# A fused attention and MLP-mixer kernel: mixing products take PSUM banks of two pools by turns, and three transposes move ahead

## The chip, the cores and the metric

The kernel runs on one core of one Trainium2 chip. The metric is device time in microseconds (us) of one execution; the time of a version is the median of its runs.

## The reference

Inputs are q, k, v of shape (8, 12, 448, 64), two gains g_q, g_k of 64 values, and four weight matrices, all float32. Per batch element ("element" below, numbered 0 to 7):

```
q_n, k_n = rmsnorm(q) * g_q, rmsnorm(k) * g_k          # per row of 64
attn = softmax(q_n @ k_n.T / 8) @ v                    # 12 heads of 448 x 448
x = attn with heads side by side                       # 448 x 768
u = x + (relu(x.T @ w_tok1) @ w_tok2).T                # token mixing, 256 wide
out = u + relu(u @ w_ch1) @ w_ch2                      # channel mixing, 1536 wide
```

## The kernel before, in words

The whole program is one pipeline over the 8 elements. While the channel mixing of element b runs on TensorE (PE), the attention of element b+1 is laid between its products, so that PE has matmuls all the time and VectorE (DVE), ScalarE (ACT) and GpSimd (POOL) work beside it. The order on those four engines is the order in which the Python code emits the work; the order of the DMA issues on SyncE (SP) is made by a scheduler. In the trace each engine, and SP's queue, works through its list in that order, so whatever stands behind a waiting instruction waits too.

**Channel mixing.** Both channel products are done with fewer, fast-matrix products than the plain way. For elements 1 to 7 the first layer is 21 units `ch1` (L1131; three groups `mp` of seven products `i`, six matmuls each, 128x224). Element 1 has a plain second layer, `plain_2` (L1185: six products, each two units of six 448-wide matmuls). Elements 2 to 7 have 15 products `ch2` (L1199; two units `x` = 0, 1 of four matmuls each), called f = 0 to 14 below. A product's result stands in a PSUM tile `m_ps`; it is read ("evicted") by DVE at L1149, L1197 or L1224, or copied by ACT at L1153, L1165 or L1220. Some evicted values are combined on DVE or POOL (L1183, `x_form`) into the moving operands of later products: the tables `X_STEPS` and `X_SLOT` say which slot of `hb` is formed after which unit, and which slot a product reads. Slot 8 is formed anew on POOL after unit (7, 1) and read by product f = 11. Weights come as "units" by DMA (L1071) into eight buffers.

**PSUM pools.** The code divides PSUM into eight tiles of 128x512, called banks here: `ps_M` (L140) has 2, for the products (`m_tile`), and `ps_S` (L138) has 4, for the scores and small transposes (`s_tile`); the other 2 are for attention's outputs, `o_ps`. A tile can only be written when the last reader of the tile before it in its bank is done.

**Attention of the next element.** For two pairs of heads and one block of 64 keys, `score` (L453) takes two `s_tile`s, runs four 64x64-tiled matmuls (L459), and ACT takes the exponential out of each tile (L463). DVE sums these (`es`, L500). q and k of a pair are loaded by SP into `qk_t` (L1563, eight DMAs a pair), squared by ACT (L1585), reduced by DVE (L1598), put through three Newton steps for the inverse root (L1620 on DVE, then L1628 to L1631, on DVE or on POOL), scaled (L1649), and turned by DVE (`turn_qk`, L436) and ACT (L439). The buffers `qk_t` are two, for even and odd pairs.

For elements 2 on, the attention of the next element comes in six blocks (`big_step`, L625), set between units of the mixing by `place` (L675) at the units `BLOCKS = (0, 6, 11, 17, 23, 31)`. A block is a run of scores and values on PE; its third list, `beside`, follows it at once, and the fourth, `between`, is spread over the units up to the next block. For block 4 (a second_block, L646) `between` holds: the turns of one more pair, the loads of the pair after next (`loads(n + 2)`, first set below), four DVE steps, the loads of `n + 3` (second set below), and two more steps. Block 5 is a first_block; its two squares read the first and the second set.

**x for the next element.** Attention's output stands transposed. `x_items(b + 1, 0)` turns half of it (three DVE transposes, `trans_x`, L878), after which `send_x` stores it to DRAM (`xs`, four DMAs, L836) and `load_x` reads it back as `x` (five DMAs, L849 and L852), all on SP; `x_items(b + 1, 1)` does the other half later. The call that puts the first half into the list of block 4 is the line

```
blocks[4][3].extend(x_items(b + 1, 0))
```

Of the kernel before, what the change touches and what calls it, by code (L numbers as in the profile page):

```python
# [83 lines left out]
def whole(ctx, tc, shifted, pre, q, k, v, g_q, g_k, moe_w_tok1, moe_w_tok2, moe_w_ch1, moe_w_ch2, out):  # L84
# [67 lines left out]
    st = dict(pre.st)  # L152
    m_tile = lambda: ps_M.tile([P, 512], F32, name="m_ps", tag="M")
    s_tile = lambda name: ps_S.tile([P, 512], F32, name=name, tag="S")

    first_ps = s_tile("first_ps")
    for _ in range(7):
# [932 lines left out]
    def put_off_done():  # L1090
        while late_work:
            late_work.pop(0)()
# [38 lines left out]
    def ch1(b, mp, i):  # L1131

        put_off_done()
        u, tu = st["uT", b], st["tu"]
        ps = m_tile()
        w = next_unit()
        q, what = PRODUCTS[i]
        for j in range(2):
            for t in range(KC):
                m = {"B11": u[:, t, 0:HS], "B21": u[:, KC + t, 0:HS], "B22": u[:, KC + t, HS:S]}.get(what)  # L1140
                if m is None:
                    m = tu[:, int(what[1]) - 1, t, :]
                nc.tensor.matmul(  # L1143
                    out=ps[:, j * HS:(j + 1) * HS], lhsT=w[:, t, j, :], rhs=m,
                    start=(t == 0), stop=(t == KC - 1))
        got = ps[:, 0:2 * HS]
        h = {name: hb[:, 2 * mp + n, 2 * o:2 * o + 2, :].rearrange("p m n -> p (m n)")
             for name, o, n in (("B11", 0, 0), ("B12", 0, 1), ("B21", 1, 0), ("B22", 1, 1))}
        add = lambda e, o, x, y: e.tensor_tensor(out=o, in0=x, in1=y, op=ALU.add)  # L1149
        relu = lambda name: put_off(lambda: nc.scalar.activation(out=h[name], in_=h[name], func=AF.Relu))  # L1150
        if i == 0:
            r[1] = r_tile(1)[:]
            nc.scalar.copy(out=r[1], in_=got)  # L1153
        elif i == 1:
            add(nc.vector, h["B11"], got, r[1])
            relu("B11")
        elif i == 2:
            r[2] = r_tile(2)[:]
            add(nc.vector, r[2], got, r[1])
        elif i == 3:  # L1160
            r[3] = r_tile(3)[:]
            add(nc.vector, r[3], got, r[2])
        elif i == 4:
            r[5] = r_tile(5)[:]
            nc.scalar.copy(out=r[5], in_=got)  # L1165
            add(nc.gpsimd, h["B22"], r[5], r[3])
            add(nc.gpsimd, r[2], r[2], r[5])
            relu("B22")
        elif i == 5:
            add(nc.vector, h["B12"], got, r[2])  # L1170
            relu("B12")
        else:
            add(nc.vector, h["B21"], got, r[3])
            relu("B21")
        if b > 1 and mp == KF // 2 - 1:
            for form in X_STEPS.get(("ch1", i), ()):
                x_form(*form)
# [7 lines left out]
    def plain_2(b, mt, half):  # L1185

        put_off_done()
        if half == 0:
            st["m"] = m_tile()
        ps, w = st["m"][:, 0:S], next_unit()[:].rearrange("p a b n -> p (a b) n")  # L1190
        for t in range(KF):
            nc.tensor.matmul(  # L1192
                out=ps, lhsT=w[:, t, :], rhs=natural(half * KF + t),
                start=(half == 0 and t == 0), stop=(half == 1 and t == KF - 1))
        if half:
            to = st["uT", b][:, mt, :]
            nc.vector.tensor_tensor(out=to, in0=to, in1=ps, op=ALU.add)  # L1197

    def ch2(b, f, x):  # L1199

        put_off_done()
        if x == 0 or ending(b) and f == NF9 - 1:
            st["m"] = m_tile()
        ps = st["m"]
        for i in range(4):
            tile_at = f * 8 + x * 4 + i
            if tile_at % 6 == 0:
                st["w"] = next_unit()[:].rearrange("p a b n -> p (a b) n")
            nc.tensor.matmul(  # L1209
                out=ps[:, x * HS:(x + 1) * HS], lhsT=st["w"][:, tile_at % 6, :], rhs=hb[:, X_SLOT[f], i, :],  # L1210
                start=(i == 0), stop=(i == 3))
        if x:
            u = st["uT", b]
            at = {(m, n): u[:, m:m + KC + 1:KC, n * HS:(n + 1) * HS] for m in range(3) for n in range(2)}
            wide = lambda a: a[:, 0:2 * HS].rearrange("p (m n) -> p m n", m=2)
            at["P"] = wide(ps)
            for eng, out, x_, op, y in C_STEPS[f] if not (ending(b) and f == NF9 - 1) else ():
                if op is None:
                    r[out] = wide(r_tile(out))
                    nc.scalar.copy(out=r[out], in_=at["P"])  # L1220
                    continue
                e = nc.gpsimd if eng == "g" else nc.vector
                get = lambda k: at[k] if k in at else r[k]
                e.tensor_tensor(  # L1224
                    out=get(out), in0=get(x_), in1=get(y), op=ALU.add if op == "+" else ALU.subtract)
        if ending(b) and f == NF9 - 1:
            part = st["uT", b][:, 1 + x * KC, 0:HS]
            nc.vector.tensor_tensor(out=part, in0=part, in1=ps[:, x * HS:(x + 1) * HS], op=ALU.add)
        for form in X_STEPS.get((f, x), ()):
            put_off(lambda form=form: x_form(*form))  # L1230
# [43 lines left out]
    def x_items(b, h):  # L1274
        return [(0.1, lambda j=j: trans_x(b, j)) for j in range(h * NC // 2, (h + 1) * NC // 2)]
# [115 lines left out]
    for b in range(B):  # L1391
        early, double = middle_items(b)
        if b == 0:
            early, last = first_items(
                tok1_items(0, 0) + x_items(0, 1) + tok1_items(0, 1) + early, double, some)
        else:
            if b > 1 and in_next(b - 1):

                y, z = sends(b - 1, y_order(b - 1)[:4]), left
                left = [y[0], y[1], z[0], y[2], z[1], y[3]]  # L1400
            run(merge(tok1_items(b, 0), left[:2]))
            begin, early = merge(tok1_items(b, 1) + early[:3 * KC], left[2:]), early[3 * KC:]
            if b == 1 and not shifted:
                run(merge(begin, sums[5:9]))
                early, begin = merge(early[:8], sums[9:]) + early[8:], []
            elif b == 1:
                early, begin = merge(begin + early[:8], sums[5:]) + early[8:], []
            if b == 1:
                form_items()
            tail, keep = (4, 2) if b == 1 else (14, 3) if ending(b) else (11, 6)  # L1410
            last, ends = double[-tail - keep:-tail], double[-tail:]
            double = double[:-tail - keep]
            early = begin + early + double
        lo = (b + AHEAD) * per + 1
        att = []
        if b + AHEAD < B and (shifted or b < 2):
            att = att_items(lo, lo + 10) + x_items(b + AHEAD, 0)
            if shifted:
                att += att_items(lo + 10, lo + per)
            elif not b:  # L1420
                step = att_step(lo + per - 1)
                att += att_items(lo + 10, lo + per - 1) + step[:5] + x_items(1, 1) + step[5:]
            else:
                run(att[:6])
                ahead, block, beside, between = big_step(BIG, False)
                att = att[6:] + att_items(lo + 10, lo + per - 1) + ahead + [block] + beside
                att += between[:6] + x_items(2, 1) + between[6:-3]
                behind_x = between[-3:]
        elif b + AHEAD < B:
            t = (b + AHEAD) * NPAIR // 2  # L1430
            blocks = [big_step(t + i // 2, i % 2) for i in range(1, NPAIR + 1)]
            blocks[4][3].extend(x_items(b + 1, 0))
            early = place(early, blocks, [near(early, at) for at in BLOCKS], in_seven(b))
        if b == 0:
            last = x_items(1, 1) * shifted + merge(last, sums[:5], turns(b, y_order(b)[2:4]))
        else:
            if b + 1 < B:
                last = merge(last, behind_x if b == 1 and not shifted else x_items(b + 1, 1))
            if b == 2 and not shifted:
                last.append((0.4, right_sums))  # L1440
            last += last_items(b, ends)
        run(merge(att, early) + last)
        if b == 0:
            load_units(0)
        left = [] if b and ending(b) else turns(b, y_order(b)[4:])
# [275 lines left out]
```

## Time and profile before

| | |
|---|---|
| median of 3 runs | 1261.07 us (1258.13 to 1261.94) |
| the profiled execution's own time | 1262.04 us |
| its span, first to last instruction | 1260.2 us |
| busy: PE, DVE, POOL, ACT | 98%, 69%, 36%, 33% |
| element 1's mixing | about 275 to 417 us |
| elements 2, 3, 4, 5 | end at about 563, 709, 855, 1001 us |

An engine's busy share is a mean over the stages; the waits of PE by the engine that ended them say what delays it. A timeline row gives start, duration, engine, line, operation, tiles and how many instructions it merges; in square brackets stands the idle time of the engine just before, and what ended it.

### The profile page before, as it was taken

The page shows a single profiled execution, that of the slowest core. Times are in us where ns is not written, and L with a number is a line of the kernel's source. Part 1 is how long each engine was busy: PE and PEld are TensorE (multiplying, and loading weights), DVE is VectorE, ACT ScalarE, POOL GpSimd, SP SyncE. Part 2 cuts the span into 40 slices and gives each one's busy share as a digit, 9 for nine tenths or more (in the row PEclk, how much of TensorE's full clock was granted, in tenths as well). Part 3 has the DMA queues.
Part 4 walks back from the last instruction along what each step waited for, and adds up shares of the span by engine and source line. Part 5 has one row for each costly group of instructions (what it writes and reads, how often), then busy time and mean ns, then how long its engine had stood idle before and what let it go on. Part 6 is the DMA issues. An engine that isn't in the chain of part 4 may idle for free.

```text
span 1260.2 us, 20320 instructions
## 1 busy us (share of the span) xinstructions
PE 1234.3 (98%) x7196; PEld 900.9 (71%) x7196; DVE 867.8 (69%) x1379; ACT 412.2 (33%) x872; POOL 452.5 (36%) x681
## 2 busy tenths in 40 slices
PE   7999999999999999999999999999999999999998
PEld 4444444457744487797778877887787887798998
DVE  6989879757774466867688487866768486656243
ACT  5664443224332144402542044312444034301210
POOL 2311651033995922334224142344133242133222
PEclk9999999999999999999999999999999999999999
DMA  9666696899799887694767767685766956486564
GB/s 206 153 172 186 183 244 162 205 259 250 211 251 208 214 204 164 130 260 93 193 154 177 190 155 177 155 200 136 191 168 131 241 119 163 120 203 172 168 174 105
DMA packets 480275, 228.39 MB, mean 181 GB/s; under 512 B 362900, under 2 KB 440084, under 8 KB 480164
## 3 DMA queue, kind: packets, MB, share of 16 engines
q1 hardware_dynamic: 472626, 211.85, 68.5%
q0 software_dynamic: 4512, 14.46, 3.9%
q8 instruction: 59, 0.97, 0.3%
q10 hardware_dynamic: 3026, 0.69, 0.3%
q14 instruction: 52, 0.43, 0.1%
HBM read 184.26 MB, written 42.66 MB: 180 GB/s over the span
## 4 chain that ended last, share of the span: by engine, by line
PE 82%; DVE 7%; SPq 4%; DMA 3%; issue 2%; ACT 2%; DVEq 0%; ACTq 0%
PE m_ps L1143 26%; PE m_ps L1209 18%; PE s_ps L459 9%; PE o_ps L532 9%; PE m_ps L1113 5%; PE m_ps L891 3%; PE t_ps L891 2%; PE m_ps L1192 2%; PE m_ps L1023 2%; PE seven_ps L977 2%; DMA qk_t<-in_k_dram 2%; PE m_ps L977 1%; SPq L1563 1%; DVE es L500 1%; SPq L412 1%
## 5 line engine op out<-in xcount | busy, mean ns | idle before, releaser
L1209 PE MATMUL m_ps<-hb,unit 128*128 128x224 f32 x1440 | 277.0, 353 | 4.5 <-DVE uT L1224 4.5
L1209 PEld LDWEIGHTS m_ps<-hb,unit 128*128 128x128 f32 x1440 | 271.3, 190 | 12.8 <-issue 7.1
L1143 PE MATMUL m_ps<-tu,unit 128*128 128x224 f32 x1008 | 202.1, 355 | 2.4 <-DVE hb L1149 1.4
L1143 PEld LDWEIGHTS m_ps<-tu,unit 128*128 128x128 f32 x1008 | 188.9, 190 | 16.8 <-issue 7.8
L463 ACT ACTIVATE e<-s_ps 128x448 f32<-128x448 f32 x294 | 138.3, 553 | 130.4 <-PE s_ps L459 130.0
L1143 PE MATMUL m_ps<-uT,unit 128*128 128x224 f32 x756 | 151.5, 354 | 0.0
L1143 PEld LDWEIGHTS m_ps<-uT,unit 128*128 128x128 f32 x756 | 142.0, 190 | 7.2 <-POOL tu L1047 2.8
L459 PE MATMUL s_ps<-qkT 64*64 64x448 f32 x1260 | 144.3, 545 | 1.1 <-ACT x L873 1.1
L532 PE MATMUL o_ps<-e,v 64*64 64x448 f32 x1148 | 130.5, 538 | 0.1
L500 DVE TENSOR_TENSOR es<-es,e 128x896 f32<-128x896 f32 x90 | 106.1, 1179 | 13.8 <-ACT e L463 9.4
L1149 POOL TENSOR_TENSOR hb<-r,r 128x448 f32<-128x448 f32 x21 | 23.9, 1140 | 218.6 <-ACT r L1165 218.6
L459 PEld LDWEIGHTS s_ps<-qkT 64*64 64x64 f32 x1260 | 45.1, 132 | 69.4 <-issue 52.5
L532 PEld LDWEIGHTS o_ps<-e,v 64*64 64x64 f32 x1148 | 45.5, 133 | 63.9 <-issue 60.8
L1628 POOL TENSOR_TENSOR nt<-rs 128x56 f32<-128x56 f32 (+1 forms) x54 | 21.7, 402 | 181.8 <-DVE rs L1620 178.6
L1224 POOL TENSOR_TENSOR uT<-uT,r 128x448 f32<-128x448 f32 x42 | 54.6, 1315 | 86.6 <-DVE r L1224 49.6
L1149 DVE TENSOR_TENSOR hb<-m_ps,r 128x448 f32<-128x448 f32 x63 | 38.8, 618 | 64.9 <-POOL r L1149 45.0
L1598 DVE TENSOR_REDUCE ms<-sq 128x28 f32<-128x896 f32 (+2 forms) x44 | 47.0, 1069 | 48.4 <-ACT sq L1585 41.4
L1150 ACT ACTIVATE hb<-hb 128x448 f32<-128x448 f32 x84 | 48.4, 576 | 91.1 <-DVE hb L1149 76.9
L324 POOL TENSOR_TENSOR raw<-raw 128x128 f32<-128x128 f32 x128 | 67.3, 545 | 20.0 <-DMA raw<-wp 15.5
L1224 DVE TENSOR_TENSOR uT<-uT,m_ps 128x448 f32<-128x448 f32 x41 | 24.9, 618 | 53.8 <-PE m_ps L1209 53.8
L1220 ACT COPY r<-m_ps 128x448 f32<-128x448 f32 x24 | 12.7, 529 | 143.4 <-PE m_ps L1209 143.4
L1113 PE MATMUL m_ps<-hb,stage 128*128 128x448 f32 x144 | 57.1, 556 | 2.0 <-ACT r L1124 1.9
(183 smaller groups left out, 1797.1 us busy)
## 6 DMA issues: line engine op xcount, KB each, us to landing
unit<-ws SPq DMA_DIRECT2D x267, 384.0 KB, 4.3
raw<-in_moe_w_ch_dram SPq DMA_DIRECT2D x72, 256.0 KB, 3.5
v<-in_v_dram SPq DMA_DIRECT2D x96, 112.0 KB, 3.6
out_dram<-turned SPq DMA_DIRECT2D x182, 56.0 KB, 2.0
xs<-xt SPq DMA_DIRECT2D x52, 168.0 KB, 4.5
qk_t<-in_q_dram SPq DMA_DIRECT2D x144, 56.0 KB, 3.5
qk_t<-in_k_dram SPq DMA_DIRECT2D x144, 56.0 KB, 3.5
x<-xs SPq DMA_DIRECT2D x39, 192.0 KB, 3.9
```

The costliest lines, as they stand in the source:

```text
L324: nc.gpsimd.tensor_tensor(out=at[o], in0=at[x], in1=at[y], op=ALU.add if op == "+" else ALU.subtract)
L459: nc.tensor.matmul(out=pss[i][rows_of(i, a), 0:S], lhsT=qkT[h, 1, k * D:(k + 1) * D], rhs=qkT[h, 0, :], start=True, stop=True)
L463: nc.scalar.activation(out=e[:, i, :], in_=pss[i][:, 0:S], func=AF.Exp)
L500: nc.vector.tensor_tensor(out=es[:], in0=(es if k > 1 else st["e", t, 0])[:], in1=st["e", t, k][:], op=ALU.add)
L532: nc.tensor.matmul(out=st["o", p][a * D:(a + 1) * D, 0:S], lhsT=vt[rows, k * D:(k + 1) * D], rhs=e[rows, :], **kw)
L891: nc.tensor.matmul(out=st["t1", h][jc][:, 0:HC], lhsT=w1_sb[:, c, jc * P:(jc + 1) * P], rhs=st["x", b, h][:, :, c, :], start=start and c = ...
L1113: nc.tensor.matmul(out=ps, lhsT=a[:, o + 2 * half, :], rhs=natural(half * KF + t) if wide else u[:, half * KC + t, :], start=(t == 0 and h ...
L1143: nc.tensor.matmul(out=ps[:, j * HS:(j + 1) * HS], lhsT=w[:, t, j, :], rhs=m, start=(t == 0), stop=(t == KC - 1))
L1149: add = lambda e, o, x, y: e.tensor_tensor(out=o, in0=x, in1=y, op=ALU.add)
L1150: relu = lambda name: put_off(lambda: nc.scalar.activation(out=h[name], in_=h[name], func=AF.Relu))
L1209: nc.tensor.matmul(out=ps[:, x * HS:(x + 1) * HS], lhsT=st["w"][:, tile_at % 6, :], rhs=hb[:, X_SLOT[f], i, :], start=(i == 0), stop=(i == 3))
L1224: e.tensor_tensor(out=get(out), in0=get(x_), in1=get(y), op=ALU.add if op == "+" else ALU.subtract)
```

## The change

First, a new function `product_tile` counts the products and hands out a tile of `ps_M` for odd counts and one of `ps_S` for even ones. `ch1`, `plain_2` and `ch2` call it where they called `m_tile` (the branch `shifted` doesn't run here). Second, `x_items(b + 1, 0)` goes to the front of the `between` list of block 4 instead of its end. Five lines are added at the top, so every line below is numbered 5 higher in the changed kernel.

```
+    def product_tile():
+
+        st["bank"] = st.get("bank", 0) + 1
+        return m_tile() if shifted or st["bank"] % 2 else s_tile("m_ps")
...
-        ps = m_tile()
+        ps = product_tile()
...
-            st["m"] = m_tile()
+            st["m"] = product_tile()
...
-            blocks[4][3].extend(x_items(b + 1, 0))
+            blocks[4][3][:0] = x_items(b + 1, 0)
```

The order of PE's instructions is the same in both. DVE in element 3, behind block 4, before (`xt` is the transposed half of x, `ms` the reduced squares, `r_22476` a product's temporary):

```order
L1183 TENSOR_TENSOR hb<-hb 128x896
L436 STREAM_TRANSPOSE qkT<-qk_t 128x448 x2
L1224 TENSOR_TENSOR r_22476<-r_22476,m_ps 128x448
L1183 TENSOR_TENSOR hb<-hb 128x896
L500 TENSOR_TENSOR es<-es,e 128x896
L1224 TENSOR_TENSOR uT<-uT,m_ps 128x2x224
L500 TENSOR_TENSOR es<-es,e 128x896
L559 STREAM_TRANSPOSE dt<-es 128x448
L560 TENSOR_REDUCE v_first<-dt 128x14
```

DVE at the same place in the changed kernel:

```order
L1188 TENSOR_TENSOR hb<-hb 128x896
L883 STREAM_TRANSPOSE xt<-uT 128x448 x3
L441 STREAM_TRANSPOSE qkT<-qk_t 128x448
L1229 TENSOR_TENSOR r_22476<-r_22476,m_ps 128x448
L441 STREAM_TRANSPOSE qkT<-qk_t 128x448
L1188 TENSOR_TENSOR hb<-hb 128x896
L1229 TENSOR_TENSOR uT<-uT,m_ps 128x2x224
L505 TENSOR_TENSOR es<-es,e 128x896 x2
```

The three transposes of x now stand ahead of the turns of the pair (L441); before, they stood behind all the rows shown and eight more. SP's queue in element 3, before, from the first set's q on (`qk_t` are the loads of q and k, `unit` the weights, `xs` the stores of x; the other two stores and the loads of x come within six rows behind these):

```order
L1563 DMA qk_t<-in_q_dram 32x14x32 x4
L1563 DMA qk_t<-in_k_dram 32x14x32 x3
L1563 DMA qk_t<-in_q_dram 32x14x32
L1071 DMA unit<-ws_17248 128x768
L1563 DMA qk_t<-in_q_dram 32x14x32
L1071 DMA unit<-ws_17248 128x768
L1563 DMA qk_t<-in_q_dram 32x14x32
L1071 DMA unit<-ws_17248 128x768
L1563 DMA qk_t<-in_q_dram 32x14x32
L1563 DMA qk_t<-in_k_dram 32x14x32 x4
L1071 DMA unit<-ws_17248 128x768
L836 DMA xs<-xt 32x42x32 x2
```

SP's queue at the same place in the changed kernel, from the first stores of x on:

```order
L841 DMA xs<-xt 32x42x32 x2
L1076 DMA unit<-ws_17248 128x768
L1568 DMA qk_t<-in_q_dram 32x14x32
L1568 DMA qk_t<-in_k_dram 32x14x32
L841 DMA xs<-xt 32x42x32
L1568 DMA qk_t<-in_k_dram 32x14x32 x2
L841 DMA xs<-xt 32x42x32
L1076 DMA unit<-ws_17248 128x768 x2
L854 DMA x<-xs 128x3x128 x3
L857 DMA x<-xs 64x3x128 x2
L1568 DMA qk_t<-in_q_dram 32x14x32 x4
L1568 DMA qk_t<-in_k_dram 32x14x32 x3
```

The stores of x stand among the first set's loads, and the five loads of x stand ahead of the second set (the last two rows; its eighth load follows behind one unit). Before, the second set stood ahead of the stores and loads of x.

More of the change, by code (lines that the diff above doesn't have):

```diff
@@ L1202, in ch2 @@
         if x == 0 or ending(b) and f == NF9 - 1:
-            st["m"] = m_tile()
+            st["m"] = product_tile()
         ps = st["m"]
```

## The prediction

> **What bounds the kernel now.** The page comes first, then PE's own waits (who waited for whom: us in total, times, longest).
>
> ```profile
> span 1260.2 us, 20320 instructions
> PE 1234.3 (98%) x7196; PEld 900.9 (71%) x7196; DVE 867.8 (69%) x1379; ACT 412.2 (33%) x872; POOL 452.5 (36%) x681
> PE first_ps L158 <- DVE ms L1598: 9.4, 1, 9.4
> PE m_ps L1209 <- DVE uT L1224: 4.5, 4, 1.1
> PE m_ps L1143 <- DVE hb L1149: 1.4, 1, 1.4
> PE m_ps L1143 <- ACT r L1153: 0.7, 1, 0.7
> PE m_ps L1192 <- DVE uT L1197: 0.6, 1, 0.6
> ```
>
> PE sets the time: of 25.9 us without a matmul, 9.4 are the start. The last four rows are products that wait for a bank, 4.5 + 1.4 + 0.7 + 0.6 = 7.2 us: about all that the first edit can win. Any new wait of PE costs its whole length. The span and 1.8 us around it make the profiled 1262.04 us, 1.0 above the median, so terms worked out on this execution are added to the median.
>
> **The banks in element 1.** A product's bank used to come free with the eviction of the product two before. Every second product now takes a score bank, freed by ACT's exponential; in return a score may have to wait for a product's eviction. Which tile follows which is in the built program's addresses; when is in the timelines of ACT and PE:
>
> ```profile
> 290.24 0.67 ACT L439 ACTIVATE qkT<-qkT,g_t 128x448 f32<-128x448 f32 x1 [8.72 <-DVE qkT L436]
> 291.28 1.82 ACT L463 ACTIVATE e<-s_ps 128x448 f32<-128x448 f32 x4
> 285.63 1.73 PE L459 MATMUL s_ps<-qkT 64*64 64x448 f32 x16
> 288.80 4.81 PE L1143 MATMUL m_ps<-tu,unit 128*128 128x224 f32 x24
> ```
>
> *Place A.* The product at 288.80 (group 0, product 3) gets the bank of the first score tile of 285.63. ACT sat behind the turn until 290.24, so the first of its four exponentials ends only at about 291.8. New wait: 3.0 us. DVE's turn doesn't depend on PE there, and nothing gives it back: what follows on DVE waits for PE's products anyway.
>
> Place B, DVE and PE, and for the pace of products a row of the chain (72 instructions are 6 products):
>
> ```profile
> 324.00 2.61 DVE L1649 TENSOR_TENSOR qk_t<-qk_t,rs 128x896 f32<-128x896 f32 x2
> 326.54 1.16 DVE L436 STREAM_TRANSPOSE qkT<-qk_t 128x448 f32<-128x448 f32 x2
> 327.62 0.58 DVE L1149 TENSOR_TENSOR hb<-m_ps,r 128x448 f32<-128x448 f32 x1
> 320.19 2.43 PE L1143 MATMUL m_ps<-tu,unit 128*128 128x224 f32 x12
> 322.56 1.73 PE L459 MATMUL s_ps<-qkT 64*64 64x448 f32 x16
> 325.72 5.07 PE L1143 MATMUL m_ps<-uT,unit 128*128 128x224 f32 x24
> 337.89 1.73 PE L532 MATMUL o_ps<-e,v 64*64 64x448 f32 x16
> 587.25 13.82 PE m_ps L1143 x72
> ```
>
> *Place B.* The product of 320.19 is now in a score bank, and DVE evicts it only at 328.20 (327.62 + 0.58), behind scaling and turning. The fourth score tile of 322.56, due at 322.56 + 3 x 0.39 = 323.7, takes that bank: 4.5 us of wait. Part comes back: the four products from 325.72 to 337.89 took 12.2 us where the pace of 2.3 makes 9.2; those waits (the 0.7 and the 1.4 are among them) are gone, since four banks lie between. Net 4.5 - 3.0 = 1.5.
>
> ```profile
> 355.50 1.73 PE L459 MATMUL s_ps<-qkT 64*64 64x448 f32 x16
> 356.01 0.95 ACT L1585 ACTIVATE sq<-qk_t 128x896 f32<-128x896 f32 x1 [4.12 <-DMA qk_t<-in_k_dram]
> 359.14 1.85 ACT L463 ACTIVATE e<-s_ps 128x448 f32<-128x448 f32 x4
> 617.21 1.74 PE L459 MATMUL s_ps<-qkT 64*64 64x448 f32 x16
> 618.23 1.85 ACT L463 ACTIVATE e<-s_ps 128x448 f32<-128x448 f32 x4 [3.34 <-PE s_ps L459]
> ```
>
> *Place C.* At 355.50 a product stands open in a score bank, so four score tiles share three, and the fourth (due 356.7) waits for the first exponential, done at 359.7: 3.0 us. ACT was held by a DMA; by then PE is 4.5 us late (3.0 + 1.5). If that DMA keeps its time the wait shrinks to what exponentials need, 0.4 (next place); if it is late too, 3.0 stays. I take 1.4, nearer the lower end, because the row shows a DMA and not PE as what ACT waits for.
>
> *Place D.* Elements 2 to 6 have one such block each, as at 617.21: fourth tile due 618.4, first exponential done at 618.8. 0.4 each; one more in element 1. The 0.6 of L1192 goes: its product no longer follows that eviction. Element 1: 3.0 + 1.5 + 1.4 + 0.4 - 0.6 = **+5.7**; bounds +4.3 and +7.3 (C at 0 or 3.0).
>
> **The gain in elements 2 to 5.** DVE, then PE:
>
> ```profile
> 675.75 1.69 DVE L878 STREAM_TRANSPOSE xt<-uT 128x448 f32<-128x448 f32 x3
> 684.02 0.61 DVE L1224 TENSOR_TENSOR uT<-uT,m_ps 128x448 f32<-128x448 f32 x1
> 684.78 24.45 PE m_ps L1209 x128
> ```
>
> Product 7 waits 1.1 us here, in each of the four elements, for an eviction that stands behind the transposes of x. Both edits remove this wait: the transposes stand earlier, and product 7 now takes a score bank. -1.1 each.
>
> **What the move does to SP.** SP's queue, three rows of DMA landings, ACT, POOL:
>
> ```profile
> 667.58 2.12 SPq L1563 DMA_DIRECT2D qk_t<-in_k_dram  x4
> 677.47 0.96 SPq L836 DMA_DIRECT2D xs<-xt  x2
> 685.59 1.45 SPq L849 DMA_DIRECT2D x<-xs  x3
> 687.08 1.24 SPq L852 DMA_DIRECT2D x<-xs  x2
> xs<-xt SPq DMA_DIRECT2D x52, 168.0 KB, 4.5
> qk_t<-in_k_dram SPq DMA_DIRECT2D x144, 56.0 KB, 3.5
> 660.97 1.08 DVE L1183 TENSOR_TENSOR hb<-hb 128x896 f32<-128x896 f32 x1
> 678.50 0.95 ACT L1585 ACTIVATE sq<-qk_t 128x896 f32<-128x896 f32 x1 [2.61 <-issue]
> 683.25 0.99 POOL L1628 TENSOR_TENSOR nt<-rs 128x56 f32<-128x56 f32 x1 [5.32 <-DVE rs L1620]
> 691.72 2.09 POOL L1183 TENSOR_TENSOR hb<-hb 128x896 f32<-128x896 f32 x1
> ```
>
> Before, the second set's last load is issued at 669.2 (667.58 + 2.12 - 0.5) and lands 3.5 later at 672.7, six us before the square of 678.50 wants it. Now it stands behind the stores and loads of x. The transposes follow L1183, 662.0 + 1.7 = 663.7, and the first store with them. From there to the last store stand nine issues at about 0.5 (2.12 for four): it goes at about 668 and lands at 672.8. The loads of x wait for that; five take 2.7, to 675.5. Then q, k, a unit and the last k, nine issues: 679.8, landing 3.5 later at **683.3**. The square moves from 678.5 to 683.3, 4.8 us.
>
> Behind it on ACT and DVE stand the reduction, the row sums, the Newton start and the eviction of product 5; on POOL the Newton steps, three adds and, at 691.72, the forming of slot 8, which product 11 reads. All move by 4.8: slot 8 is done at 698.6 instead of 693.8. Product 11 starts at 684.78 + 4 x 3.06 = 697.0 (128 instructions are 8 products, 24.45/8) and, without the old wait, would start at 695.9. It starts at 698.8: 1.8 later than before, the gain of 1.1 used up. A delay up to 2.0 costs nothing and keeps the 1.1; one of 7, if landings lengthen in the fuller queue, costs 4.0. Products 6 to 10 are not held: six banks let PE run ahead of DVE. Per element 1.8 + 0.4 = 2.2; elements 2 to 5 **+8.8**, bounds 4 x (0.4 - 1.1) = -2.8 and 4 x 4.4 = +17.6. Element 6, which loads no further pairs: +0.4.
>
> **The clock.** A wait of PE in element 0, and the granted clock (third number from the end) from 213 to 216 us:
>
> ```profile
> 212.21 7.97 PE L1113 MATMUL m_ps<-hb,stage 128*128 128x448 f32 x16 [1.89 <-ACT r L1124]
> 213.00:216.00 3.00, 3.00 (x5) 1.34 (x5) 2.97 (x2) 1.02 (x2) 2.03 (x2) 0.50 1.03 248
> 204.04 6.28 PE L1113 MATMUL m_ps<-hb,stage 128*128 128x448 f32 x16
> ```
>
> After a wait of 1.9 us the clock was granted at half and the same 16 matmuls took 1.7 us longer; waits of 1.4 and 1.1 had no such echo. Places A and B are longer than 1.9, so 1.7 each: **+3.4**. Product 11's four new waits (1.8 + 1.1 = 2.9) may add 6.8 more, C 1.7; I leave them to the upper end, since one row shows that it can happen, not that it always does. The Trainium skill, "TensorE: Matmul & The Clock Gate", section "HAM oscillation — how this bites in real kernels", states that only idle gaps over about 3.4 us bring the clock down; by that rule B alone pays and the sum is 1.7 less. The trace's 1.89 us speaks against so high a bound.
>
> Sum: 5.7 + 8.8 + 0.4 + 3.4 = 18.3; 1261.07 + 18.3 = **1279.4 us**, slower by 1.5%.
>
> **Rivals.**
> 1. *The second set isn't late*: stores land sooner, or POOL's chain has more room than the rows say. Then elements 2 to 5 give -2.8, and 5.7 - 2.8 + 0.4 = 3.3 makes 1264.4; with the clock 1267.8. For it: the median landing hides how fast a quiet queue is. Against: three dependent transfers stand in one line. Decides at a delay of 2.0.
> 2. *Faster*: the banks only take waits away. If ACT and DVE reach places A, B and C before PE, -7.2 remains: 1253.9. Against: ACT's 8.72 us behind DVE's turn at A and the backlog at B are not PE's doing. The Trainium skill, "Perfetto Trace Analysis", section "Optimization Strategy", says that a gap repeating on the engine that should be saturated can mean too little PSUM for the next tile; the four equal waits of 1.1 look like that, and by it alone 4.5 is won, 1256.6.
> 3. *The set is later still* and each of the four waits slows the clock: 5.7 + 4 x (4.4 + 1.7) + 0.4 + 3.4 = 33.9, 1295.0.
>
> **How the numbers follow.** A measurement here tells about 0.3% (3.8 us) from nothing. The forecast 0.62 (its own range 1271 to 1288), rival 1 0.20 (half of it within 0.3%), rival 2 0.06 (0.05 faster, 0.01 same), rival 3 0.12. Slower 0.62 + 0.12 + 0.10 = 0.84, same 0.10 + 0.01 = 0.11, faster 0.05. The range runs from rival 1 to nearly rival 3: 1264 to 1292.
>
> **What would show it.** Right: PE waits of about 3 us for ACT's exponential at the fourth product and 4.5 for DVE's L1154 at a score in element 1; none for DVE at product 7; in elements 2 to 5 the second square held by a `qk_t` load until some 5 us later than before, and PE waiting for POOL's L1188 at product 11; a half clock behind the long waits. Wrong: that square at its old place, or no wait of PE above 2 us in element 1.

## The result, and the profile after

| | before | after |
|---|---|---|
| median | 1261.51 us (1258.13 to 1262.93, 4 runs) | 1298.22 us (1296.65 to 1305.89, 4 runs) |
| ratio | | 1.0307 (95%: 1.0261 to 1.0353) |
| profiled execution: time, span | 1262.04, 1260.2 us | 1296.65, 1294.8 us |

The change makes the kernel slower by 36.7 us: the sign of the forecast (+18.3), twice its size, and above its range. The page of the changed kernel, and then PE's waits (us in total, times, longest):

```profile
span 1294.8 us, 20275 instructions
...
PE 1248.0 (96%) x7196; PEld 907.3 (70%) x7196; DVE 878.6 (68%) x1379; ACT 414.3 (32%) x872; POOL 448.5 (35%) x681
```

```profile
PE m_ps L1214 <- POOL hb L1188: 10.1, 4, 3.1
...
PE m_ps L1214 <- DVE r L1229: 6.7, 4, 2.0
PE s_ps L464 <- DVE hb L1154: 3.5, 1, 3.5
PE m_ps L1148 <- ACT e L468: 2.8, 1, 2.8
PE t_ps L903 <- DMA x<-xs: 2.4, 1, 2.4
PE m_ps L1197 <- DMA unit<-wp: 2.2, 1, 2.2
...
PE s_ps L464 <- ACT e L468: 0.4, 1, 0.4
```

The four waits of product 7 (4.5 us) are gone, as are the 1.4, 0.7 and 0.6 of element 1. In their place stand seven kinds of new waits, 28.1 us. The first two rows are products 11 and 10 of elements 2 to 5, the next two places B and A. The two DMA rows, at the end of element 1, stand nowhere in the prediction.

Where the time went shows in the length of each element, from its first matmul of token mixing (L891 before, L896 after) to that of the next, read from the timelines of PE (us):

| kernel | 0 | 1 | 2 | 3 | 4 | 5 | 6 | 7, end |
|---|---|---|---|---|---|---|---|---|
| before | 176.6 | 162.9 | 146.6 | 145.8 | 145.7 | 145.7 | 142.3 | 117.4 |
| after | 174.1 | 174.0 | 157.5 | 150.3 | 150.4 | 150.7 | 143.0 | 117.7 |
| first edit alone (run 1) | 175.3 | 174.5 | 152.4 | 145.3 | 145.3 | 145.3 | 144.2 | 117.4 |
| second edit alone (run 2) | 174.2 | 163.5 | 155.3 | 153.7 | 153.5 | 153.4 | 142.1 | 117.4 |
| SP's order in element 1 kept (run 9) | 175.0 | 168.0 | 146.2 | 145.3 | 145.3 | 145.7 | 143.1 | 117.4 |
| product 7 only (run 11) | 174.1 | 164.0 | 145.3 | 144.4 | 144.4 | 144.4 | 142.2 | 117.3 |

Element 1 is 11.1 longer, element 2 10.9, elements 3 to 5 4.5 to 5.0 each. Element 2 has the same 4.6 as its neighbours, the wait of 2.4 for x, and two stretches of half clock of 1.7 each. Element 0 is 2.5 shorter because before's profiled execution had a wait of 1.9 and a half clock there; of the other profiled executions only that of run 12 has this half clock.

**Element 3, where the second set is late.** One row of before to line the two up (the products behind the second block), then after: PE, SP's queue, ACT, POOL.

```profile
677.33 6.32 PE L1209 MATMUL m_ps<-hb,unit 128*128 128x224 f32 x32
```

```profile
697.55 15.40 PE L1214 MATMUL m_ps<-hb,unit 128*128 128x224 f32 x80
714.54 3.29 PE L1214 MATMUL m_ps<-hb,unit 128*128 128x224 f32 x16 [1.59 <-DVE r L1229]
720.73 5.57 PE L1214 MATMUL m_ps<-hb,unit 128*128 128x224 f32 x28 [2.89 <-POOL hb L1188]
```

```profile
683.87 0.97 SPq L841 DMA_DIRECT2D xs<-xt  x2
...
688.14 2.12 SPq L1568 DMA_DIRECT2D qk_t<-in_k_dram  x2
690.30 0.48 SPq L841 DMA_DIRECT2D xs<-xt  x1
...
694.37 1.44 SPq L854 DMA_DIRECT2D x<-xs  x3
...
697.14 2.17 SPq L1568 DMA_DIRECT2D qk_t<-in_q_dram  x4
...
701.44 0.44 SPq L1568 DMA_DIRECT2D qk_t<-in_k_dram  x1
```

```profile
705.39 0.95 ACT L1590 ACTIVATE sq<-qk_t 128x896 f32<-128x896 f32 x1 [8.90 <-DMA unit<-ws]
718.62 2.06 POOL L1188 TENSOR_TENSOR hb<-hb 128x896 f32<-128x896 f32 x1
```

Counted from the products behind the block, the square stood at 678.50 - 677.33 = 1.2 us and stands now at 705.39 - 697.55 = 7.8: 6.7 late. SP shows why, row by row: the stores of x, a gap until they have landed, the five loads of x, and only then the set, whose last load is issued at 701.4. (The square's row names a unit's load, which was issued next; the square doesn't read units, and in run 2 the row of the same square names the set's `qk_t`.) POOL's slot 8 is done at 720.7, and PE starts product 11 in that moment.

**The end of element 1.** SP's queue before and after, and what its raw weight loads waited for in 360 to 425 us (before, L308; after, L313). These raw weights are what POOL combines into the units of the later elements:

```profile
372.15 1.95 SPq L1563 DMA_DIRECT2D qk_t<-in_q_dram  x4
...
377.01 4.60 SPq L836 DMA_DIRECT2D xs<-xt  x4
...
388.91 1.45 SPq L849 DMA_DIRECT2D x<-xs  x3
...
406.74 1.29 SPq L308 DMA_DIRECT2D raw<-wp  x2
```

```profile
376.04 0.56 SPq L1076 DMA_DIRECT2D unit<-wp  x1
385.61 0.96 SPq L313 DMA_DIRECT2D raw<-wp  x2
...
389.07 2.33 SPq L1568 DMA_DIRECT2D qk_t<-in_q_dram  x4
...
394.78 8.88 SPq L841 DMA_DIRECT2D xs<-xt  x4
...
410.69 1.45 SPq L854 DMA_DIRECT2D x<-xs  x3
```

```profile
SPq L308 <- DMA ws<-raw: 9.2, 2, 5.4
```

```profile
SPq L313 <- DMA ws<-raw: 18.3, 3, 9.0
```

A raw load that stood behind x (406.74) now stands ahead of the pair's loads, and SP sits for 9.0 us (376.6 to 385.6) until its buffer has been written out. The loads, the stores and x come 17 to 22 us later, while PE is only 4 to 8 us later there. The diff moves nothing here; SP's order is the scheduler's, and it puts this load elsewhere once products of element 1 take other banks (run 7 below). Over all the kernels of this document: in the five in which this load, or half of it, stands ahead of the pair's loads, element 1 takes 174.0 to 177.4 us; in the nine in which it stands behind x, 162.8 to 169.6.

### The profile page after: what moved, and what is told of

Read it like the earlier page. It is cut to its first block, busy times and chain, and to the rows that moved or that the text cites. A ratio compares the mean times of both kernels' runs of the same rounds, so it can differ in the third digit from the quotient of the medians.

```text
span 1294.8 us, 20275 instructions
## 1 busy us (share of the span) xinstructions
PE 1248.0 (96%) x7196; PEld 907.3 (70%) x7196; DVE 878.6 (68%) x1379; ACT 414.3 (32%) x872; POOL 448.5 (35%) x681
## 4 chain that ended last, share of the span: by engine, by line
PE 74%; DVE 7%; DMA 5%; POOL 5%; SPq 4%; issue 2%; ACT 2%; DVEq 0%; ACTq 0%; POOLq 0%
PE m_ps L1148 25%; PE m_ps L1214 16%; PE s_ps L464 9%; PE o_ps L537 8%; PE m_ps L1118 3%; PE m_ps L896 2%; PE t_ps L896 2%; PE m_ps L1028 2%; PE seven_ps L982 2%; PE m_ps L982 1%; POOL raw L329 1%; DMA xs<-xt 1%; SPq L1568 1%; DVE es L505 1%; POOL uT L1229 1%
## 5 line engine op out<-in xcount | busy, mean ns | idle before, releaser
L1214 PE MATMUL m_ps<-hb,unit 128*128 128x224 f32 x1440 | 281.6, 357 | 16.8 <-POOL hb L1188 10.1
L1148 PEld LDWEIGHTS m_ps<-tu,unit 128*128 128x128 f32 x1008 | 190.4, 191 | 17.4 <-issue 7.8
L464 PE MATMUL s_ps<-qkT 64*64 64x448 f32 x1260 | 156.6, 547 | 5.0 <-DVE hb L1154 3.5
L1148 PEld LDWEIGHTS m_ps<-uT,unit 128*128 128x128 f32 x756 | 142.3, 190 | 7.0 <-POOL tu L1052 2.9
L537 PE MATMUL o_ps<-e,v 64*64 64x448 f32 x1148 | 138.9, 543 | 0.1
L464 PEld LDWEIGHTS s_ps<-qkT 64*64 64x64 f32 x1260 | 48.5, 132 | 78.9 <-issue 51.5
L537 PEld LDWEIGHTS o_ps<-e,v 64*64 64x64 f32 x1148 | 48.3, 134 | 63.1 <-issue 60.1
L329 POOL TENSOR_TENSOR raw<-raw 128x128 f32<-128x128 f32 x128 | 64.4, 522 | 18.9 <-DMA raw<-wp 14.4
L1590 ACT ACTIVATE sq<-qk_t 128x896 f32<-128x896 f32 x36 | 34.2, 951 | 89.1 <-DMA qk_t<-in_k_dram 58.7
L1197 PE MATMUL m_ps<-hb,unit 128*128 128x448 f32 x144 | 55.5, 543 | 2.2 <-DMA unit<-wp 2.2
## 6 DMA issues: line engine op xcount, KB each, us to landing
xs<-xt SPq DMA_DIRECT2D x52, 168.0 KB, 3.9
```

Of the source, the lines that this page charges most:

```text
L329: nc.gpsimd.tensor_tensor(out=at[o], in0=at[x], in1=at[y], op=ALU.add if op == "+" else ALU.subtract)
L464: nc.tensor.matmul(out=pss[i][rows_of(i, a), 0:S], lhsT=qkT[h, 1, k * D:(k + 1) * D], rhs=qkT[h, 0, :], start=True, stop=True)
L537: nc.tensor.matmul(out=st["o", p][a * D:(a + 1) * D, 0:S], lhsT=vt[rows, k * D:(k + 1) * D], rhs=e[rows, :], **kw)
L1148: nc.tensor.matmul(out=ps[:, j * HS:(j + 1) * HS], lhsT=w[:, t, j, :], rhs=m, start=(t == 0), stop=(t == KC - 1))
L1197: nc.tensor.matmul(out=ps, lhsT=w[:, t, :], rhs=natural(half * KF + t), start=(half == 0 and t == 0), stop=(half == 1 and t == KF - 1))
L1214: nc.tensor.matmul(out=ps[:, x * HS:(x + 1) * HS], lhsT=st["w"][:, tile_at % 6, :], rhs=hb[:, X_SLOT[f], i, :], start=(i == 0), stop=(i == 3))
```

## The experiments

Theory: three separate causes, namely places A and B, late transfers at the end of element 1, and the second set behind x in elements 2 to 5. Rivals: the banks do all of it; the move does all of it; the late transfers merely follow from A and B. Ratios are to the kernel before, with 95% intervals.

**1. The first edit alone.** Against the changed kernel:

```
-            blocks[4][3][:0] = x_items(b + 1, 0)
+            blocks[4][3].extend(x_items(b + 1, 0))
```

> The first edit alone: products take banks of both pools by turns, x's half stays at the end of its list. My theory has three separate causes: score-bank waits in element 1 (A and B, each with a half clock behind it), late transfers at the end of element 1, and the second qk_t set behind x's stores and loads in elements 2 to 5. The first two belong to this edit and the third doesn't. So element 1 is again some 13 us longer up to the start of element 2 (waits of about 3 us for ACT L468 and 3.5 us for DVE L1154), elements 2 to 5 each get about 0.7 us shorter (the old product-7 wait of 1.1 gone, 0.4 paid at a score), and no product waits for POOL: about 1269 us (1265 to 1274). Rival 1, the banks do all of it (six banks let PE run ahead until POOL's slot 8 is late): also elements 2 to 5 lose 4.5 us each, 1290 us or more, with waits of 3 us for POOL at product 11. Rival 2, the late transfers at the end of element 1 come from the move: element 1 is only 7 us longer, about 1263 us.

1277.18 us, ratio 1.0115 (1.0092 to 1.0139). Element 1 pays in full (table), elements 3 to 5 win 0.4 to 0.5 each, and no product waits for POOL. So the banks don't make slot 8 late. The time lies above the expected span: elements 1 and 2 together cost 11.6 + 5.8 = 17.4 where 13 was expected.

**2. The second edit alone.** Against the changed kernel:

```
-        return m_tile() if shifted or st["bank"] % 2 else s_tile("m_ps")
+        return m_tile()
```

> The second edit alone: x's half at the front of the list, products with their two banks as before. My theory: the second square is again 6 to 7 us late because its loads stand behind x's stores and loads, slot 8 with it, and product 11 waits for POOL; elements 2 to 5 each get 3.5 to 4 us longer, element 1 doesn't change, and one or two of the four waits bring a half clock of 1.7: about 1278 us (1274 to 1284). Rival 1, the banks do all of it: elements 2 to 5 within 1 us of before, 1257 to 1263 us. Rival 3, the square is late but with two banks PE is held by evictions instead, from the products behind the late square on, and more of it: 6 us per element, 1286 us.

1293.87 us, ratio 1.0262 (1.0241 to 1.0283): the third alternative (rival 3), and dearer still, 7.7 to 8.7 in each of elements 2 to 5. Its waits of PE and, in element 3, PE's row:

```profile
PE m_ps L1214 <- DVE uT L1229: 27.8, 4, 7.6
```

```profile
697.57 4.72 PE L1214 MATMUL m_ps<-hb,unit 128*128 128x224 f32 x13 [6.83 <-DVE uT L1229]
```

Product 7 waited 1.1 us for an eviction behind the square, so every microsecond of lateness is added to that wait: the square is 5.7 late here, and 1.1 + 5.7 = 6.8. Each of these four waits also has two stretches of half clock behind it, 6.8 us in which PE works for about 4.4, so that about 2.2 of the 8 are clock. Six banks move the wait on to products 10 and 11 and take the cost from about 8 to 4.7: in the changed kernel the first edit shields it from part of the second.

**3. x's loads behind the second set.** Against the changed kernel, in `trans_x`:

```
-            start, step, load = {(1, 1): (2.0, 0.5, 9.0), (2, 1): (0.0, 0.25, 6.0)}.get((b, half), (2.0, 2.0, 12.0))
+            start, step, load = {(1, 1): (2.0, 0.5, 9.0), (2, 1): (0.0, 0.25, 6.0)}.get((b, half), (2.0, 2.0, 18.0 if b > 2 and not half else 12.0))
```

> The changed kernel, with only the five loads of x's first half given later, so that on SP they stand behind the second qk_t set; its four stores stay where they are. My theory: the set lands early enough again, the square returns to within 2 us of its old place, the waits at products 10 and 11 in elements 2 to 5 (3.7 + 1.1 us each) are gone with their half clocks: 1298 - 4 x 4.8 - 3 = about 1276 us (1272 to 1281). Rival A, the stores (they wait for the transposes on DVE) hold the set just as well: less than half of it comes back, 1288 us or more. Rival B, the DVE transposes in front of the turns are what is late: no gain, 1297 us, and the square isn't held by a DMA.

1285.63 us, ratio 1.0192 (1.0174 to 1.0210): between the theory and rival A. Element 3, PE and ACT, and PE's waits:

```profile
696.82 18.43 PE L1214 MATMUL m_ps<-hb,unit 128*128 128x224 f32 x96
701.54 0.95 ACT L1590 ACTIVATE sq<-qk_t 128x896 f32<-128x896 f32 x1 [5.88 <-DMA x<-xs]
```

```profile
PE m_ps L1214 <- POOL hb L1188: 5.8, 4, 2.1
```

The square stands at 701.54 - 696.82 = 4.7: 3.5 late, where it was 6.7. The loads of x are about half of the lateness; the rest must be the stores or the transposes.

**4. Stores and loads of x behind the set.** The same line of `trans_x`, against the changed kernel:

```
-            start, step, load = {(1, 1): (2.0, 0.5, 9.0), (2, 1): (0.0, 0.25, 6.0)}.get((b, half), (2.0, 2.0, 12.0))
+            start, step, load = {(1, 1): (2.0, 0.5, 9.0), (2, 1): (0.0, 0.25, 6.0)}.get((b, half), (22.0, 2.0, 32.0) if b > 2 and not half else (2.0, 2.0, 12.0))
```

> The changed kernel with the stores and the loads of x's first half given later, so that on SP the whole second set of qk_t stands ahead of both, as in the kernel before; the three transposes on DVE stay at the front. If the set's place on SP is the whole cost of the move, elements 2 to 5 do as with the first edit alone: the 1.7 us that each still lost with only the loads behind are gone, no product waits for POOL, and the time is that of the first edit alone, about 1277 us (1274 to 1280). Rival, the transposes in front of the turns and of an eviction cost something themselves: 1281 us or more, with PE still waiting for POOL L1188.

1275.22 us, ratio 1.0119 (1.0104 to 1.0134), that of the first edit alone. Elements 3 to 5 take 145.3 to 145.4. PE and ACT in element 3:

```profile
689.39 25.80 PE L1214 MATMUL m_ps<-hb,unit 128*128 128x224 f32 x135
691.04 0.95 ACT L1590 ACTIVATE sq<-qk_t 128x896 f32<-128x896 f32 x1 [2.89 <-DVE ms L1603]
```

The square is 0.5 late, and no product of elements 2 to 5 waits. With six banks the transposes on DVE, which are what was moved, cost nothing; the DMAs that they drag along on SP cost everything.

**5. The first edit without element 1.** Against run 1, with the element kept in `st["mixing"]`:

```
-        return m_tile() if shifted or st["bank"] % 2 else s_tile("m_ps")
+        return m_tile() if shifted or st["mixing"] < 2 or st["bank"] % 2 else s_tile("m_ps")
```

> The first edit in the mixing of elements 2 to 7 only (element 1 keeps its two banks), x's half at the end of its list. My theory: the costs of element 1 are gone and only the small gain is left, 4 x (1.1 - 0.4) - 0.4 = 2.4 us: about 1259 us (1256 to 1262), no product 7 waiting for DVE. Rival 1, banks do all of it: slower than before, 1275 us or more. Rival C, PE's old wait at product 7 only moves on to a later product: 1261.5 us, no difference.

1261.31 us, ratio 1.0002 (0.9989 to 1.0014): no difference. The wait at product 7 is gone, but elements 3 to 5 take 145.3, where product 7 alone in a score bank makes 144.4 (run 11): 0.9 go back at the scores (at place D of element 3, from the first score to the next product, 7.0 us here and 6.2 in run 11; no single gap there is long enough to be listed as a wait), and the whole gain of the first edit is 0.4 us per element.

**6. Places A and B alone.** Against run 1; `st["bank"]` counts from 1 in each element here and in runs 7 to 12 but for run 10:

```
-        return m_tile() if shifted or st["bank"] % 2 else s_tile("m_ps")
+        return m_tile() if shifted or not (st["bank"] in (4, 14) if st["mixing"] == 1 else 0) else s_tile("m_ps")
```

> The kernel before with two products of element 1 in a score bank and no others: the fourth and the fourteenth, those of places A and B. SP's queue keeps its order there but for one unit that stands a little earlier. If A and B cost what their waits cost, PE waits 3.0 us for ACT L468 and 4 to 4.5 for DVE L1154, some 2 us of later waits come back (0.7 and 1.4 in the profile of before), and each has a half clock of 1.7 behind it: 3.0 + 4.5 - 2.1 + 3.4 = +8.8, about 1270 us (1267 to 1272), and no PE wait for a DMA at the end of element 1. Rival 1, the late transfers there follow from any lateness of PE: another 5 us, 1275 us. Rival 2, the half clocks are not caused by the waits: 1266.5 us.

1266.43 us, ratio 1.0047 (1.0033 to 1.0062): just under the range, and at the time that rival 2 gave. The waits stand as expected:

```profile
PE s_ps L464 <- DVE hb L1154: 4.3, 1, 4.3
PE m_ps L1148 <- ACT e L468: 3.0, 1, 3.0
```

No wait for a DMA follows, so lateness of PE alone doesn't make the transfers late. In the trace element 1 is 6.7 longer; only one of the two waits had a half clock behind it, of twice the usual length. So rival 2's reason is out though its time came: the clock costs 3.4, and about 3.0 + 4.3 + 3.4 - 6.7 = 4.0 came back later, not 2.1.

**7. SP's other order without A and B.** The same line with three other products:

```
+        return m_tile() if shifted or not (st["bank"] in (8, 10, 12) if st["mixing"] == 1 else 0) else s_tile("m_ps")
```

> The kernel before with the eighth, tenth and twelfth product of element 1 in a score bank and no others: neither place A nor B is touched, but SP's queue comes out as in the first edit alone in one respect: half of a raw weight load and two loads of v stand ahead of a pair's loads and of x. If that order makes the end of element 1 late, PE waits there for a unit or for x, 2 to 5 us with its half clock: about 1266 us (1263 to 1270). Rival, the late transfers only follow from A and B: 1261 us, with no PE wait for a DMA.

1276.69 us, ratio 1.0127 (1.0112 to 1.0141): far more than expected, without A or B. Waits of SP (360 to 420 us) and of PE, DVE, and the piece of the chain in which the stores of x land:

```profile
SPq L313 <- DMA ws<-raw: 15.1, 2, 9.2
```

```profile
PE m_ps L1197 <- DVE uT L1202: 12.6, 1, 12.6
```

```profile
416.85 1.09 DVE L1604 TENSOR_REDUCE ms<-sq 128x28 f32<-128x896 f32 x1 [22.63 <-ACT sq L1591]
```

```profile
392.43 16.22 DMA xs<-xt
```

The raw load (half of it, two issues) holds SP, the stores of x take 16.2 us to land (9.2 in the kernel before, 11.0 in the changed one; why is open), the rest of the pair's loads stand behind x's, DVE waits 22.6 us for the square, and the eviction behind it lets PE wait 12.6. The three products themselves have no new wait, but no run changes SP's order with every bank as before. With six banks in the plain second layer, as in the change, PE gets past that eviction and waits for the unit and for x instead.

**8. The first edit with SP's order kept.** Products 8, 10 and 12 and the plain second layer of element 1 keep two banks:

```
+        return m_tile() if shifted or not ((st["bank"] in (2,4,6,14,16,18,20) if st["mixing"] == 1 else st["bank"] % 2 == 0)) else s_tile("m_ps")
```

> The first edit alone, except that in element 1 the eighth, tenth and twelfth product and the six of the plain second layer keep their two banks; places A and B are in it. With these left out SP's queue in element 1 comes out as before (but for one unit), so the raw weight load no longer stands ahead of a pair's loads and x. If that order is what element 1's end paid in the first edit alone, only A and B are left (+5.3 as measured with them alone) and 0.3 us per element are won in elements 2 to 5: about 1265 us (1263 to 1268), with no PE wait for a unit or for x at the end of element 1. Rival, banks by turns make that end late in some other way: 1272 us or more.

1276.92 us, ratio 1.0114 (1.0094 to 1.0133): missed. Element 1 did as expected (169.6 us, no wait for a DMA), but elements 2 to 5 took 147.7 to 148.8, because this edit counted the products anew in each element and so gave the score banks to the other half of them:

```profile
PE s_ps L464 <- DVE r L1229: 3.4, 4, 0.9
```

Which half takes the score banks is worth 2.4 us per element.

**9. The same with the half of the changed kernel.** `st["bank"] % 2 == 1` at the end of that condition.

> As the run with SP's order kept, but with the products of elements 2 to 7 by turns in the parity of the changed kernel (the run before had the other one, which cost 2.0 us in each of elements 2 to 5: scores waited for DVE L1229). Element 1 as in that run: 6.6 us longer with A and B, and no PE wait for a DMA at its end; elements 2 to 5 now 0.4 us shorter each: 1262 + 6.6 - 2.5 (element 0 as it comes) - 1.2 = about 1265 us (1263 to 1268). Rival, the first edit costs elements 2 to 5 something even so: 1270 us or more.

1266.16 us, ratio 1.0038 (1.0024 to 1.0052), as expected. Against run 1 it is 11 us: what the place of that raw load costs in the first edit, the plain layer's banks included.

**10. The whole change without element 1.** Run 5 with x's half at the front, `blocks[4][3][:0] = x_items(b + 1, 0)`.

> The whole change but for element 1, whose products keep their two banks (SP's order there as before). If the parts add up, this is the changed kernel less what the first edit alone cost, and that cost is all in element 1: 1298.2 - 16 = about 1282 us (1279 to 1285), elements 2 to 5 longer by 4.7 each, with waits of some 1.6 us for DVE L1229 at product 10 and 3 us for POOL L1188 at product 11. Rival, the late square in elements 2 to 5 hangs on the late start that element 1 leaves: 1270 us or less.

1288.42 us (1282.54 to 1289.64), ratio 1.0198 (1.0170 to 1.0226): above the expected range. PE's waits are those of the changed kernel:

```profile
PE m_ps L1214 <- POOL hb L1188: 10.1, 4, 2.9
PE m_ps L1214 <- DVE r L1229: 7.3, 4, 2.1
```

So the rival is out: the late square needs no late start. The 6 us over the expectation are clock: one execution with a mean granted clock of 0.998 took 1282.54, the others (0.992 to 0.994) 1287.96 to 1289.64. This profiled execution had six half-clock stretches in elements 2 to 5, the changed kernel's two, at 1.7 us each; without them elements 2 to 5 take 150.0 to 150.5.

**11. Product 7 alone.** The twenty-ninth product of an element is f = 7; x's half at the end:

```
+        return m_tile() if shifted or not (st["bank"] == 29 and 1 < st["mixing"] < 6) else s_tile("m_ps")
```

> The kernel before with a single product of elements 2 to 5, the one that waited 1.1 us for DVE (f = 7), in a score bank. No score has to wait for it, since its eviction is long done when the bank comes round. If that wait was PE's own, 4 x 1.1 us go: about 1257 us (1256 to 1259), no PE wait for DVE L1229 left. Rival, the wait moves on to the next product, which waits for the same DVE queue: 1261 us. SP's queue may come out in another order, and then the same loss as elsewhere may hide the gain.

1255.40 us, ratio 0.9963 (0.9951 to 0.9975): 0.4% faster than the kernel before. Elements 2 to 5 are 1.3 to 1.4 shorter each, no product of theirs waits, and SP's order is that of before, issue for issue.

**12. Product 7, and two of element 1.** The same condition with `or st["mixing"] == 1 and st["bank"] in (17, 18)`.

> Product f = 7 of elements 2 to 5 in a score bank, as before, and the seventeenth and eighteenth product of element 1 too, which waited 0.7 and 1.4 us for their banks. SP's order is that of the kernel before. If those waits are PE's own and don't move on, 1 to 2 us more go: about 1254 us. Rival, they move to the next product: 1255.5 us, as without them. A difference of 1 us is at the edge of what five rounds tell.

1258.41 us, where before took 1262.76 beside it: ratio 0.9969 (0.9956 to 0.9981), no gain over run 11 that this could tell. Of the two waits 0.6 is left, and another came:

```profile
PE o_ps L537 <- DMA v<-in_v_dram: 2.5, 1, 2.5
```

## Why the prediction was right in direction and half the size

- *Element 1's sum: the step that failed.* It has only bank waits and their clock, 5.7 + 3.4, and SP's queue there is put at nothing without a reason: the prediction followed that queue in elements 2 to 5, where the diff moves x, and not in element 1, where the diff moves nothing. The order of SP differs there. With three other products and two banks in the second layer this costs 15.5 us (run 7), and 11.0 of the first edit's 16 us go with it (runs 1 and 9).
- *Places A and B: right waits, too dear.* Waits of 2.8 and 3.5 us stand where 3.0 and 4.5 were forecast. Alone, with their clock, they make a ratio of 1.0047 (run 6), about 5.9 us, where 3.0 + 1.5 + 3.4 was forecast.
- *Place C: at its lower end.* 0.4 for 1.4. *Place D: twice as dear.* 0.9 per element (runs 5 and 11) for 0.4.
- *The second set: right mechanism, undersized.* The first stores went at 683.9 as worked out (663.7 moved by the 20.2 that PE is later there). The last store went 690.3 - 683.9 = 6.4 us behind the first and not 4.3, since the issues between them waited too: two loads took 2.1 instead of 1.0. That makes the square 6.7 late, not 4.8. Behind it the chain was worked out rightly: from square to slot 8 it takes 15.3 us before and after. Product 11 starts 720.73 - 20.2 - 697.0 = 3.5 later than before, not 1.8: with the 0.9 of the scores about 4.4 per element, where 2.2 was forecast, and 4.5 to 5.0 in the table. (In element 5 product 11 waits only 1.2; a half clock of 1.7 just before it takes the rest.)
- *"Both edits remove this wait": shown for one.* Product 7 doesn't wait where it takes a score bank; with the move alone its wait grew from 1.1 to 6.8 (run 2), because the eviction stands behind the square, and the square was late.
- *"Products 6 to 10 are not held": wrong, and without effect.* Product 10 waits 1.6 us for the eviction of product 6, which stands behind the late reduction. Product 11 waits for POOL whatever product 10 does.
- *The clock: right kind, too few.* Two slow stretches were in the sum; the profiled execution has five (A, B, the wait for x, and two in elements 2 to 5), 8.5 us and not 3.4.
- *The rivals.* Rival 1 (the set isn't late) is out by the rows above. Rival 2 (faster) had one true core: the four waits of 1.1 are PE's own, and run 11 takes them. By the Trainium skill, "Perfetto Trace Analysis", section "Optimization Strategy", a repeating gap can mean too little PSUM; run 11 agrees, with one more bank for one product, while banks for all products bring back nothing (run 5). Rival 3 came nearest, 1295.0, in part by luck: its 4.4 for the later set was right, but only two of the four elements had a half clock, and element 1 brought the rest.

Put together from the table, without element 0: the banks of element 1 cost about 5 (run 9), SP's order about 11, the second set with the scores and two half clocks 20.5, element 6 0.8, in all 37.3; by the table elements 1 to 7 are 37.2 longer. For the same four the forecast had 9.1, nothing, 8.8 and 0.4. That the sum came out at half, and not at less, is partly luck, since the banks were put 4 too high.

Not settled: by which of its rules the scheduler puts the raw load elsewhere. The runs show only that three products in other banks are enough for it.

## What to carry to other kernels

A scheduler that orders a DMA queue can answer to edits that touch no DMA, as here: after a change of buffers compare the whole queue, and look for a load that waits for its buffer ahead of loads that are due. A step that is moved drags its transfers along, and here they, not the step, were the cost. And where one wait repeats, try the spare buffer at that one step first: here eighteen products per element in score banks won 0.4 us, a single one 1.4.

## What the runs showed of the hardware that was not expected

The half clock comes in stretches of 3.41 us on a fixed grid: in the changed kernel they start at 289.6, 330.6, 433.0, 569.5 and 1016.6 us, which lie 12, 30, 40 and 131 times 3.413 apart. Stretches of that grid in the changed kernel (PE busy, then the granted clock):

```profile
286.20:289.60 3.40, 0.58 (x6) 1.00 1.01 236
289.60:293.00 3.40, 3.40 (x11) 0.50 0.96 294
716.30:719.70 3.40, 1.54 (x9) 1.00 0.61 151
719.70:723.10 3.40, 2.37 (x12) 1.00 0.91 142
```

Before a slow stretch PE idled 2.0 to 2.9 us of the 3.4 in this kernel, and 1.89 in the kernel before; the wait of 2.89 before 720.73 is as long, but a border of the grid cuts it into 1.8 and 1.1, and no slow stretch follows. In the other runs idle times up to 1.94 in one stretch had none behind them, and 1.88 and 1.99 had one; the 1.94 is what a border left of the wait of 3.0 at place A in run 6. So, as far as these runs go, about 1.9 us of idling inside one stretch decides, and where a wait falls on the grid is luck: nearly the same waits cost run 10 six slow stretches in elements 2 to 5 and the changed kernel two. The changed kernel's slowest run, 9.2 us over its fastest, had a mean granted clock of 0.986 against 0.993: worked out, 0.007 x 1300 / 1.7 = 5 more such stretches. In runs 1, 6 and 10 a slow stretch was followed by a second one after less idling (0.4 to 0.9), and one in run 3 came after 1.3; what counts there stays open. The Trainium skill, "TensorE: Matmul & The Clock Gate", section "HAM oscillation — how this bites in real kernels", names idle gaps of over about 3.4 us as what to avoid. The waits of 1.9 to 3.0 here had half clocks behind them, so the measurement decides against so high a bound.
